# Six row-maximum tasks of attention A, one to a group instead of two in the third group

## The chip, the cores and the metric

The kernel runs on one core of a Trainium2 chip. The metric is the device time of one execution in microseconds (us). The kernel before was timed three times; the figure to beat or to miss is the median of those runs. Two runs of this kernel can be told apart when they differ by about 0.2%, or 3.9 us.

## The reference

Two attentions over the same input x (2048 tokens, 512 channels, 32 heads of 16) are mixed by a gate per token:

```python
q, k, v = heads(x @ wq), heads(x @ wk), heads(x @ wv)        # A, in 4 segments of 512 tokens
for s in range(4):
    logits = qs @ ks.T * scale + mask                        # causal inside the segment
    o = g * (phi(qs) @ M) / (phi(qs) @ z) + (1 - g) * softmax(logits) @ vs
    M, z = M + phi(ks).T @ vs, z + phi(ks).sum()             # memory of the segments before
a = concat(o) @ wo
b = softmax(q @ k.T * scale) @ v @ wob                       # B, its own weights, all 2048 keys
out = gate * a + (1 - gate) * b
```

The change touches only the two softmaxes, and in them only the row maxima that are taken off the logits before the exponential.

## The kernel before

**Units and slots.** After a stage of projections, the attention runs as 32 slots, k = 0 to 31. A slot holds one unit of B (number 32+k: four heads, 512 queries, all 2048 keys) and one unit of A (number k: four heads, one segment of 512 by 512, causal). It is written as 37 groups. Groups 0 to 31 are B's, groups 32 to 36 are A's five.

**What a group does.** `t_group` (L516) multiplies keys by queries into two PSUM banks (`tb`, `mb`; three banks in turn), and ScalarE takes the exponential of each into `raw` (L537); for A, GpSimd then clears the part above the diagonal (L540). A head pair takes rows 0 to 63 or rows 64 to 127 of TensorE's array, so two such matmuls in different halves run side by side. `pvs` (L856) then issues the multiplication of older exponentials by V into the bank `pvb` (`pv`, L543). `pvb` is shared: when a unit is finished its sums are copied out (`fin_copy`, L556) before the next unit's first `pv` may write there. B's sums are copied by ScalarE in group 33 (L562), A's by VectorE in group 0 of the slot after (L560).

**The maxima.** They must be known before a unit's exponentials, so they are found one slot ahead by multiplying queries by keys a second time and letting VectorE reduce the product. B's unit has 32 tasks `s_b` (L467), one between the two matmuls of each of 32 consecutive groups, from group 20 of one slot to group 19 of the next. Each makes two matmuls into one score tile and one reduction over 1024 values (L476). A's unit has six tasks `s_a` (L442), in the order of `ST_A`, with 512, 512, 384, 384, 256 and 128 keys; the last two take both head pairs at once. Each adds the causal mask by small matmuls (L456) and ends in one reduction (L460, or L462 for the last two). The task with 512 values in its reduction is called (0, None), the one before it (1, None).

**The two score tiles.** All tasks, `s_b` and `s_a`, take the two score tiles `sbk` in strict turn (`rot("s", SBK)`). So a task's matmuls have to wait until the reduction of the task two before it is done.

**Order.** Every engine runs its instructions in the order in which they are written. The table `plan` says which tasks a group gets; in the main loop a B group hands its tasks to `t_group`, which runs them between its two matmuls, and an A group runs them after `t_group` and before `pvs`. In slots 9 to 31, group 1 also holds one output projection `out_mm` (L615, 12 matmuls, L619); it has no `pv`. Slot 30 gives the last tasks for A; slot 31 has none.

```python
ST_A = [(3, 0), (3, 1), (2, 0), (2, 1), (1, None), (0, None)]      # L665
b = rot("s", SBK)                                                   # L445 in s_a, L471 in s_b
plan.setdefault((k, 2 * NT + n - (n > 2)), []).append(todo(s_a, k + 1, *t))   # L933, NT = 16
```

Of the kernel before, what the change touches and what calls it, by code (L numbers as in the profile page):

```python
# [23 lines left out]
NT = SEQ // 128  # L24
# [10 lines left out]
def gated_mix_kernel(ctx, tc, xt, wq, wk, wv, wo, beta, wqkv, wob, gate_w, out):  # L35
# [370 lines left out]
    def load_q(u):  # L406
        kd, qd, c = UN[u]
        load_qk(q_of(u), kd, 0, qd, c)

    def load_ka(u):  # L410
        kd, qd, c = UN[u]
        load_qk(KA[u % 2], kd, 1, qd, c)

    def load_kb(k, c=None):
        dst = KB[k % 3] if c is None else KB[k % 3][:, :, c * C:(c + 1) * C]
        load_qk(dst, "B", 1, k % 8, c)
# [6 lines left out]
    def load_vb(g):  # L423
        v_src(VB[g % 2], "B", g % 4, None)
# [55 lines left out]
    def m_chain(k):  # L480
        mx = pair_max(k)
        if k == 1:
            nc.vector.memset(mx[:, 0], 0.0)
        if k < 32:
            nc.vector.tensor_reduce(mx[:, 1], MXB.pop(32 + k).rearrange("q j p i c -> q (j p) i c"), axis=AX.X,
                                    op=OP.max)
        else:
            nc.vector.memset(mx[:, 1], 0.0)
        del MX[k]
        mx = mx.rearrange("q u h i -> q (u h i)")  # L490
        m8 = M8[k] = W.tile([128, 2, 32], FT, name="m8")
        hi = W.tile([128, 32], FR, name="mhi")
        nc.vector.tensor_scalar(hi, mx, -1.0, None, op0=OP.mult)
        nc.vector.tensor_copy(m8[:, 0], hi)
        nc.vector.scalar_tensor_tensor(m8[:, 1], mx, -1.0, hi, op0=OP.mult, op1=OP.subtract)
# [20 lines left out]
    def t_group(u, n, banks, between=()):  # L516


        kd, qd, c = UN[u]
        bs = [bank(banks) for _ in range(2)]  # L520
        c0 = 0
        for it, hs in (((n // 2, (n % 2 * 2, n % 2 * 2 + 1)),) if kd == "B" else GA[n]):
            q0 = 128 * it if kd == "A" else 0
            w = C - q0
            pn = it if kd == "B" else it % 2
            for j, h in enumerate(hs):
                if j:
                    for f in between:
                        f()
                r = slice(64 * j, 64 * j + 64)  # L530
                nc.tensor.matmul(bs[j][:, c0:c0 + w], k_of(u, h // 2)[r, 128 * it:128 * it + 128],  # L531
                                 q_of(u)[r, h // 2, q0:], start=True, stop=True)
                PT[u, it, h] = PTILE[pn % 2][:, 2 + j if (kd, it) == ("A", 2) else h][:, c0:c0 + w]
            c0 += w
        for j in range(2):
            pt = PTILE[pn % 2][:, 2 + j if (kd, n) == ("A", 4) else hs[j]]
            nc.scalar.activation(pt, bs[j], AF.Exp, scale=SCALE)  # L537
            if kd == "A":
                m = pt[:, :128] if n < 2 else pt.rearrange("p (a t) -> p a t", a=4)[:, ::3 if n < 4 else 2]
                nc.gpsimd.affine_select(out=m, in_=m, pattern=[[1, 128]] if n < 2 else [[0, 2], [1, 128]],  # L540
                                        compare_op=OP.is_ge, fill=0.0, base=0, channel_multiplier=-1)
# [119 lines left out]
    def todo(fn, *a):  # L661
        return lambda: fn(*a)
# [90 lines left out]
    for blk in range(16):  # L753
# [9 lines left out]
        n = blk + 1 + (c == 2)  # L763
# [74 lines left out]
    def late():  # L838
        proj.close()
        L = AT["L"] = ctx.enter_context(tc.tile_pool(name="late", bufs=1))  # L840
        VB[1] = L.tile([128, NT, 8, E + 1], FT, name="vb1")
        AT["o"] = [L.tile([128, 4, 2, C], FT, name=f"o{n}") for n in range(2)]
        AT["wh"] = L.tile([128, 4, 2, DM], FR, name="wh")
        AT["wl"] = L.tile([128, 4, 2, DM], FR, name="wl")
        AT["d"] = [L.tile([128, C], FT, name=f"d{n}") for n in range(2)]
        AT["oh"] = L.tile([128, 4, 2, 128], FR, name="oh")
        AT["ol"] = L.tile([128, 4, 2, 128], FR, name="ol")
        for p in range(2):
            set_aux(KB[2][:, p], 0)
# [4 lines left out]
    NG = 2 * NT + 5  # L854

    def pvs(k, n):  # L856

        ua, ub = k, 32 + k
        if n == 0:
            if k:  # L860
                pv(ua - 1, 2)
                fin_copy(ua - 1)
        elif k == 31 and n < 2 * NT:
            if n % 2 and n > 1:
                pv(ub, n // 2 - 1)
        elif 2 <= n < 2 * NT + 2:
            pv(ub, n // 2 - 1, n % 2 * 256, n % 2 * 256 + 256)
            if n == 2 * NT + 1:
                fin_copy(ub)
        elif n > 2 * NT + 1:  # L870
            m = n - 2 * NT - 2
            if m < 2:
                pv(ua, 0, 256 * m, 256 * m + 256)
            else:
                pv(ua, 1)
                pv(ua, 3)
# [13 lines left out]
    def beside(k, it):  # L890

        for f, it0, u in ((fin_load, NT + 1, 32 + k), (fin_rec, 5, 31 + k), (fin_bc, 6, 31 + k),
                          (fin_load, 1, k - 1), (fin_rec, 6, k - 1), (fin_bc, S_LAST + 2, k - 1)):
            if it == it0 and (k or it0 > NT):
                f(u)
        c, j = divmod(k - 1, 8)
        if k and j % 2:
            for kd, it0 in (("B", 9), ("A", 13)):
                if it == it0:
                    fin_norm(kd, j // 2, c)  # L900
        if k >= 8 and k % 2 == 0 and it == NT + 2:
            out_split(k // 8 - 1, k // 2 % 4)
        if (k, it) == (31, 4):
            grest = AT["grest"] = AT["o"][0][64:, 0, 0]
            nc.sync.dma_start(grest, GD[3 * C:].rearrange("(o t) -> o t", o=1).to_broadcast([64, C]))
        if (k, it) == (31, 9):
            grest = AT["grest"]
            nc.vector.tensor_scalar(grest, grest, nh[64:, 3:4], None, op0=OP.mult)
        if (k, it) == (31, NT + 2):
            fin_rec(63)  # L910
        if k == 31 and it == 13:
            o = AT["o"][1][:64, 3, 0]
            nc.gpsimd.tensor_tensor(o, o, AT["d"][0][:64], op=OP.mult)
        if k == 31 and it < 8 and it % 2 == 0:
            for a in range(2):
                tail_split(it // 2, slice(0, 3), a)
# [3 lines left out]
    plan = {}  # L920

    def spread(tasks, gs):
        for n, p in enumerate(gs):
            plan.setdefault(p, []).extend(tasks[len(tasks) * n // len(gs):len(tasks) * (n + 1) // len(gs)])

    for k in range(31):
        if k:
            spread([todo(s_b, 33 + k, *t) for t in (sorted(ST_B, key=lambda t: t[2]) if k == 1 else ST_B)],
                   [(k - 1, n) for n in range(2 * S_FIRST, 2 * NT)] + [(k, n) for n in range(2 * S_LAST)])
        else:  # L930
            spread(st33[EARLY:], sorted([(0, n) for n in range(2 * S_LAST)] + [(0, 2 * n) for n in range(4)]))
        for n, t in enumerate(ST_A):
            plan.setdefault((k, 2 * NT + n - (n > 2)), []).append(todo(s_a, k + 1, *t))  # L933

    for k in range(32):
        ua, ub = k, 32 + k
        banks = T3 + [b[:, 0] for b in SBK] * (k == 31)
        for n in range(NG):
            it = n // 2 if n < NG - 1 else NT + 2
            mid = plan.pop((k, n)) if n < 2 * NT and (k, n) in plan else []  # L940
            t_group(*(ub, n) if n < 2 * NT else (ua, n - 2 * NT), banks, mid)
            for f in plan.get((k, n), []) + ex[k][0].get(n, []):
                f()
            pvs(k, n)
            for f in ex[k][1].get(n, []):
                f()
            if n % 2 == 0 and n < NG - 1:
                continue
            beside(k, it)
            if it == S_LAST:  # L950
                m_chain(k + 1)
            if it == 4 and not k:
                late()
            if it == 4 and not k:
                load_q(ub + 2)
                for c in range(NC4):
                    load_kb(2, c)
            if it == NT and k < 29:
                load_q(ub + 3)
                load_kb(k + 3)  # L960
            if it == 6 and k < 31:
                load_q(ua + 1)
                load_ka(ua + 1)
                if (ua + 1) % 2 == 0:
                    load_va(ua + 1)
            if it == 9:
                if k % 2 == 0 and k < 30:
                    load_vb(k // 2 + 1)
                if 1 <= k <= 4:
                    load_wo(k - 1)  # L970
# [55 lines left out]
```

## Time and profile before

| | us |
|---|---|
| median of three runs | 1951.39 (1950.05 to 1952.76) |
| the profiled execution | 1949.85 |
| its span, first to last instruction | 1948.1 |
| TensorE busy | 1926.0 (99%) |
| VectorE busy | 1628.4 (84%) |
| ScalarE busy | 1436.2 (74%) |
| GpSimd busy | 277.0 (14%) |
| granted TensorE clock, mean | 0.997 |

Slots 1 to 8 last about 47.5 us each, slots 9 to 30 about 49.7 us. Matmuls are pipelined and their ends are modelled, so a busy TensorE may hide short waits; those are read from the start times of the instructions, and from the idle time of the weight loads (PEld), which the profile lists with the engine that ended it.

### The profile page before, as it was taken

The page shows a single profiled execution, that of the slowest core. Times are in us where ns is not written, and L with a number is a line of the kernel's source. Part 1 is how long each engine was busy: PE and PEld are TensorE (multiplying, and loading weights), DVE is VectorE, ACT ScalarE, POOL GpSimd, SP SyncE. Part 2 cuts the span into 40 slices and gives each one's busy share as a digit, 9 for nine tenths or more (in the row PEclk, how much of TensorE's full clock was granted, in tenths as well). Part 3 has the DMA queues.
Part 4 walks back from the last instruction along what each step waited for, and adds up shares of the span by engine and source line. Part 5 has one row for each costly group of instructions (what it writes and reads, how often), then busy time and mean ns, then how long its engine had stood idle before and what let it go on. Part 6 is the DMA issues. An engine that isn't in the chain of part 4 may idle for free.

```text
span 1948.1 us, 43539 instructions
## 1 busy us (share of the span) xinstructions
PE 1926.0 (99%) x17485; PEld 931.7 (48%) x17485; DVE 1628.4 (84%) x1798; ACT 1436.2 (74%) x2699; POOL 277.0 (14%) x497
## 2 busy tenths in 40 slices
PE   7999999999999999999999999999999999999999
PEld 5887777434444444444444444444444444444445
DVE  6135765899999999999999999999999999999942
ACT  4233333688888888888888888888888888888884
POOL 5200000011120101111111111111111111101022
PEclk9999999999999999999999999999999999999999
DMA  7666656744443445454544354534444444434111
GB/s 217 163 208 185 189 194 179 174 95 117 99 115 87 104 87 105 87 115 87 115 88 115 85 115 87 115 87 115 87 112 91 98 97 96 103 88 110 47 50 58
DMA packets 163790, 222.49 MB, mean 114 GB/s; under 512 B 39916, under 2 KB 90556, under 8 KB 157828
## 3 DMA queue, kind: packets, MB, share of 16 engines
q1 hardware_dynamic: 159284, 211.41, 44.0%
q0 software_dynamic: 3248, 8.03, 2.2%
q8 instruction: 138, 2.26, 0.5%
q14 instruction: 64, 0.52, 0.1%
q10 hardware_dynamic: 1056, 0.26, 0.1%
HBM read 147.95 MB, written 68.16 MB: 111 GB/s over the span
## 4 chain that ended last, share of the span: by engine, by line
PE 95%; DVE 2%; DMA 2%; SPq 0%; ACT 0%; issue 0%; DVEq 0%; ACTq 0%
PE pvb L553 33%; PE tb L531 17%; PE sbk L474 12%; PE mb L531 9%; PE tb L304 5%; PE sbk L452 3%; PE tb L619 2%; PE mb L304 2%; PE sbk L287 1%; PE tb L287 1%; PE pvb L304 1%; PE mb L619 1%; DMA pd<-pvs 1%; PE sbk L456 1%; PE mb L287 1%; PE pvb L287 1%
## 5 line engine op out<-in xcount | busy, mean ns | idle before, releaser
L476 DVE TENSOR_REDUCE mxb<-sbk 128x2 f32<-128x1024 f32 x1024 | 1222.0, 1222 | 57.7 <-PE sbk L474 25.4
L537 ACT ACTIVATE raw<-tb 128x512 f32<-128x512 f32 x1555 | 887.7, 598 | 147.3 <-PE tb L531 103.6
L553 PE MATMUL pvb<-raw,vb 128*17 128x256 f32 (+1 forms) x8072 | 639.9, 388 | 0.0
L537 ACT ACTIVATE raw<-mb 128x512 f32<-128x512 f32 x782 | 467.6, 598 | 73.0 <-PE mb L531 47.3
L474 PE MATMUL sbk<-xh,qb 64*128 64x512 f32 x1344 | 475.2, 445 | 2.9 <-DMA xh<-dB 2.0
L531 PE MATMUL tb<-qb,xh 64*128 64x512 f32 x872 | 353.2, 443 | 0.0
L553 PEld LDWEIGHTS pvb<-raw,vb 128*17 128x17 f32 x8072 | 134.9, 95 | 344.0 <-issue 338.7
L474 PE MATMUL sbk<-kb,qb 64*128 64x512 f32 x704 | 239.4, 444 | 0.2 <-DVE mxb L476 0.2
L531 PEld LDWEIGHTS tb<-qb,xh 64*128 64x128 f32 x872 | 146.4, 185 | 176.6 <-issue 89.7
L540 POOL TENSOR_SCALAR_AFFINE_SELECT raw<-raw 128x256 f32<-128x256 f32 (+1 forms) x320 | 116.1, 363 | 694.8 <-ACT raw L537 687.0
L531 PE MATMUL mb<-qb,xh 64*128 64x512 f32 x445 | 198.8, 447 | 0.0
L474 PEld LDWEIGHTS sbk<-xh,qb 64*128 64x128 f32 x1344 | 189.1, 185 | 8.0 <-DVE mxb L476 4.3
L531 PE MATMUL tb<-qb,kb 64*128 64x512 f32 x470 | 191.9, 446 | 0.8 <-DVE st L314 0.8
L460 DVE TENSOR_REDUCE mx<-sbk 128x2 f32<-128x768 f32 (+1 forms) x128 | 136.7, 1090 | 22.9 <-PE sbk L456 18.5
L531 PEld LDWEIGHTS mb<-qb,xh 64*128 64x128 f32 x445 | 82.1, 184 | 94.9 <-issue 50.8
L531 PEld LDWEIGHTS tb<-qb,kb 64*128 64x128 f32 x470 | 79.2, 184 | 98.9 <-issue 53.1
L593 POOL TENSOR_TENSOR o<-o,d 128x512 f32<-128x512 f32 x31 | 39.8, 1284 | 549.1 <-DMA d<-rd 505.0
L531 PE MATMUL mb<-qb,kb 64*128 64x512 f32 x234 | 104.0, 445 | 0.0
L474 PEld LDWEIGHTS sbk<-kb,qb 64*128 64x128 f32 x704 | 95.2, 184 | 5.7 <-issue 3.2
L553 PE MATMUL pvb<-raw,va 128*17 128x256 f32 (+2 forms) x1280 | 94.7, 384 | 0.8 <-ACT pvs L562 0.8
L452 PE MATMUL sbk<-ka,qa 64*128 64x256 f32 (+3 forms) x512 | 87.9, 358 | 1.1
L311 ACT ACTIVATE st<-tb 128x512 fp32r<-128x512 f32 x33 | 19.8, 599 | 82.5 <-DVE phi L310 45.5
(284 smaller groups left out, 1851.5 us busy)
## 6 DMA issues: line engine op xcount, KB each, us to landing
xh<-dB SPq DMA_DIRECT2D x38, 512.0 KB
vb<-vdB SPq DMA_DIRECT2D x16, 1088.0 KB
dB<-st SPq DMA_DIRECT2D x64, 256.0 KB
dA<-st SPq DMA_DIRECT2D x64, 256.0 KB
pd<-pvs SPq DMA_DIRECT2D x64, 256.0 KB
kb<-dB SPq DMA_DIRECT2D x22, 512.0 KB
xh<-dB SPq DMA_DIRECT2D x38, 256.0 KB
qb<-dB SPq DMA_DIRECT2D x64, 128.0 KB
```

Source lines behind the costliest of these rows:

```text
L287: nc.tensor.matmul(b, lhs, WV[wi][:, k, :], start=n == 0, stop=n == 11)
L304: nc.tensor.matmul(b, WS[ws][w][wi][:, k, :], (XH, XL)[xi][c][:, k, :], start=n == 0, stop=n == 11)
L452: nc.tensor.matmul(b[:, j, c0:c0 + n], q_of(u)[r, p, i * 128:(i + 1) * 128], k_of(u, p)[r, :n], start=True, stop=False)
L460: nc.vector.tensor_reduce(m[:, :, p, i], b[:, :, :n], axis=AX.X, op=OP.max)
L474: nc.tensor.matmul(b[:, j], q_of(u)[r, p, i * 128:(i + 1) * 128], k_of(u, p)[r, kc * C:(kc + 1) * C], start=True, stop=True)
L476: nc.vector.tensor_reduce(MXB[u][:, :, p, i, kc], b, axis=AX.X, op=OP.max)
L531: nc.tensor.matmul(bs[j][:, c0:c0 + w], k_of(u, h // 2)[r, 128 * it:128 * it + 128], q_of(u)[r, h // 2, q0:], start=True, stop=True)
L537: nc.scalar.activation(pt, bs[j], AF.Exp, scale=SCALE)
L540: nc.gpsimd.affine_select(out=m, in_=m, pattern=[[1, 128]] if n < 2 else [[0, 2], [1, 128]], compare_op=OP.is_ge, fill=0.0, base=0, channe ...
L553: nc.tensor.matmul(PVB[32 * h:32 * h + E + 1, q0 + lo:q0 + hi], vt[:, it, 4 * q + h, :], pt[:, lo:hi], start=it == 0 and lo == 0, stop=it ...
L593: nc.gpsimd.tensor_tensor(o, o, d, op=OP.mult)
L619: nc.tensor.matmul(b, (AT["oh"], AT["ol"])[oi][:, g, a], (AT["wh"], AT["wl"])[wi][:, g, a], start=n == 0, stop=n == 11)
```

## The change

A's six tasks of a slot were put into groups 32, 33, 34, 34, 35, 36. Now they go into 32, 33, 34, 35, 36 and group 0 of the next slot, for the slots 0 to 29; slot 30 keeps the old places. A B group may thus hold two tasks. It hands only the last one of its list to `t_group`; the rest run after `t_group`. In group 0 the last of the list is the `s_b` task, so `s_a`'s (0, None) follows it. Where a group of slot 0 holds two `s_b` tasks (groups 0, 2, 4, 6, 7 and 19), they now run in the other order, one between the two matmuls and one behind them.

```diff
         for n, t in enumerate(ST_A):
-            plan.setdefault((k, 2 * NT + n - (n > 2)), []).append(todo(s_a, k + 1, *t))
+            at = (k, 2 * NT + n - (n > 2)) if k == 30 else divmod(k * NG + 2 * NT + n, NG)
+            plan.setdefault(at, []).append(todo(s_a, k + 1, *t))
...
-            mid = plan.pop((k, n)) if n < 2 * NT and (k, n) in plan else []
+            mid = [plan[k, n].pop()] if n < 2 * NT and (k, n) in plan else []
```

On TensorE in group 34 of slot 13, before, from the last matmul of `t_group` to the start of group 35 (`sbk_114` and `sbk_115` are the two score tiles, `va` is V of A; the mask's matmuls are left out):

```order
L531 MATMUL mb<-qa_74,ka_72 128x128
L452 MATMUL sbk_114<-ka_71,qa_73 128x384 x2
...
L452 MATMUL sbk_115<-ka_71,qa_73 128x384 x2
...
L553 MATMUL pvb<-raw_86,va_76 17x256 x4
L531 MATMUL tb_111<-qa_74,ka_72 128x384
```

The same place in the changed kernel, on to the first matmuls of group 35's task:

```order
L531 MATMUL mb<-qa_74,ka_72 128x128
L452 MATMUL sbk_114<-ka_71,qa_73 128x384 x2
...
L553 MATMUL pvb<-raw_86,va_76 17x256 x4
L531 MATMUL tb_111<-qa_74,ka_72 128x384
...
L452 MATMUL sbk_115<-ka_71,qa_73 128x384 x2
```

The second task has moved behind the first `pv` of A and behind group 35's score matmuls; the two after it move on by one group each.

On TensorE at the start of slot 14, before, from the end of group 36 to the output projection in group 1:

```order
L553 MATMUL pvb<-raw_86,va_76 17x128 x4
L531 MATMUL tb_110<-qb_69,xh_88 128x512
L474 MATMUL sbk_114<-kb_89,qb_70 128x512 x2
L531 MATMUL mb<-qb_69,xh_88 128x512
L553 MATMUL pvb<-raw_86,va_76 17x256 x4
L531 MATMUL tb_111<-qb_69,xh_88 128x512
L474 MATMUL sbk_115<-kb_89,qb_70 128x512 x2
L531 MATMUL tb_110<-qb_69,xh_88 128x512
L619 MATMUL mb<-wh,oh 128x512 x4
```

And in the changed kernel, where L452 on `ka_71` is the task (0, None) that came over:

```order
L553 MATMUL pvb<-raw_86,va_76 17x128 x4
L531 MATMUL tb_110<-qb_69,xh_88 128x512
L474 MATMUL sbk_115<-kb_89,qb_70 128x512 x2
L531 MATMUL mb<-qb_69,xh_88 128x512
L452 MATMUL sbk_114<-ka_71,qa_73 128x128 x2
...
L553 MATMUL pvb<-raw_86,va_76 17x256 x4
L531 MATMUL tb_111<-qb_69,xh_88 128x512
L474 MATMUL sbk_115<-kb_89,qb_70 128x512 x2
L531 MATMUL tb_110<-qb_69,xh_88 128x512
L619 MATMUL mb<-wh,oh 128x512 x4
```

Group 0 has two tasks, and the `s_b` tasks of groups 0 and 1 now take the same score tile (`sbk_115`), with only (0, None) between them; before, they took different ones.

On VectorE at the start of a slot, as the difference (L462 into `mx` is A's reduction, L476 into `mxb` is B's, L560 copies A's finished sums out of `pvb`):

```order
 L462 TENSOR_REDUCE mx<-sbk_114 128x4
-L462 TENSOR_REDUCE mx<-sbk_115 128x4
-L476 TENSOR_REDUCE mxb<-sbk_114 128x2
+L476 TENSOR_REDUCE mxb<-sbk_115 128x2
+L462 TENSOR_REDUCE mx<-sbk_114 128x4
 L560 COPY pvs<-pvb 128x512
 L476 TENSOR_REDUCE mxb<-sbk_115 128x2
```

The last reduction of A's tasks has moved behind the first of B's in the next slot and stands directly ahead of the copy. The orders of ScalarE, GpSimd and the DMA queues are the same in both kernels.

## The prediction

> **What bounds the kernel now.** I read the page first, then the groups of instructions, then two whole slots as windows, and last the timelines of single engines around one slot boundary. The page:
>
> ```profile
> PE 1926.0 (99%) x17485; PEld 931.7 (48%) x17485; DVE 1628.4 (84%) x1798; ACT 1436.2 (74%) x2699; POOL 277.0 (14%) x497
> PE 95%; DVE 2%; DMA 2%; SPq 0%; ACT 0%; issue 0%; DVEq 0%; ACTq 0%
> ```
>
> TensorE (PE) is busy throughout and carries 95% of the chain that ended last. Two slots as windows (columns: length, then busy time of PE, PEld, VectorE, ScalarE, GpSimd), slot 13 first, then slot 3:
>
> ```profile
> 982.98:1032.71 49.73, 49.70 (x508) 20.90 (x505) 46.10 (x47) 42.05 (x78) 6.02 (x12) 1.00 0.38 84
> 498.33:545.79 47.46, 47.42 (x497) 19.15 (x494) 45.73 (x47) 40.76 (x76) 7.35 (x15) 1.00 0.48 99
> ```
>
> VectorE (DVE) works 46.10 of 49.73 us in slot 13, but 45.73 of 47.46 in slot 3, which has no output projection: there the two engines are almost level. So the question is only where TensorE waits for VectorE. The groups of weight loads tell how much of that there is:
>
> ```profile
> L452 PEld LDWEIGHTS sbk<-ka,qa 64*128 64x128 f32 x512 | 52.1, 185 | 5.9 <-DVE mx L460 4.2 <-issue 0.9
> L474 PEld LDWEIGHTS sbk<-xh,qb 64*128 64x128 f32 x1344 | 189.1, 185 | 8.0 <-DVE mxb L476 4.3 <-DMA xh<-dB 2.3 <-issue 0.6
> ```
>
> A's tasks wait 4.2 us in all for a reduction of A (L460), about 0.14 in each of the 31 slots that hold tasks; that is what the change can take away. B's tasks (L474) wait 4.3 us for one of B in this group.
>
> **The boundary of slots 13 and 14.** The rows of TensorE that begin a step (start, length, instruction), groups 34, 35, 36 of slot 13 and 0, 1 of slot 14, which start at 1027.58, 1029.43, 1030.94, 1032.71 and 1033.93:
>
> ```profile
> 1027.58 0.44 PE L531 MATMUL tb<-qa,ka 64*128 64x384 f32 x1
> ...
> 1028.15 0.23 PE L456 MATMUL sbk<-cmask,crows 64*128 64x64 bf16 x4
> 1028.42 0.45 PE L452 MATMUL sbk<-ka,qa 64*128 64x384 f32 x2
> 1028.71 0.23 PE L456 MATMUL sbk<-cmask,crows 64*128 64x64 bf16 x4
> 1028.87 0.63 PE L553 MATMUL pvb<-raw,va 128*17 128x256 f32 x8
> 1029.43 0.50 PE L531 MATMUL tb<-qa,ka 64*128 64x384 f32 x4
> ...
> 1030.38 0.63 PE L553 MATMUL pvb<-raw,va 128*17 128x256 f32 x8
> 1030.94 0.38 PE L531 MATMUL mb<-qa,ka 64*128 64x256 f32 x1
> ...
> 1031.28 0.22 PE L452 MATMUL sbk<-ka,qa 64*128 64x128 f32 x2
> ...
> 1031.72 1.06 PE L553 MATMUL pvb<-raw,va 128*17 128x384 f32 x16
> 1032.71 0.49 PE L531 MATMUL tb<-qb,xh 64*128 64x512 f32 x1
> ...
> 1033.37 0.63 PE L553 MATMUL pvb<-raw,va 128*17 128x256 f32 x8
> 1033.93 0.50 PE L531 MATMUL tb<-qb,xh 64*128 64x512 f32 x1
> ...
> 1034.59 0.50 PE L619 MATMUL mb<-wh,oh 128*128 128x512 f32 x1
> ```
>
> What VectorE, ScalarE and GpSimd do there:
>
> ```profile
> 1033.47 1.23 DVE L476 TENSOR_REDUCE mxb<-sbk 128x2 f32<-128x1024 f32 x1 [0.94 <-PE mb L531]
> 1027.85 0.60 ACT L562 ACTIVATE pvs<-pvb 128x512 f32<-128x512 f32 x1
> 1030.69 0.90 POOL L540 TENSOR_SCALAR_AFFINE_SELECT raw<-raw 128x256 f32<-128x256 f32 x2 [0.78 <-ACT raw L537]
> ```
>
> **Groups 34 to 36 get shorter by 0.42 us.** From the mask's matmuls to `pv` it is 0.16 (1028.71 to 1028.87). Without its second task group 34 could therefore start `pv` at 1028.15 + 0.16 = 1028.31 rather than 1028.87. But this `pv` is A's first write to `pvb`, and ScalarE copies B's sums out until 1027.85 + 0.60 = 1028.45. With 0.05 for the hand-over (below) it starts at 1028.50: 0.37 gained, and 0.19 of what the task and its wait cost is not. The copy hangs on exponentials of group 33, which the change does not move, so I take 1028.50; 1028.31 is the other end. Group 35 lasts 1.51 now; with the (2, 1) task it is as group 34 with one task and no wait, 0.73 to `pv` (1027.58 to 1028.31) and 0.56 for it (1028.87 to 1029.43): 1.29, a gain of 0.22. Group 36 gets (1, None): 0.95 to `pv`, as now in group 35 (1029.43 to 1030.38), and 0.99 for it (1031.72 to 1032.71): 1.94 instead of 1.77, a loss of 0.17. Together -0.37 - 0.22 + 0.17 = -0.42. A possible new wait: `pv` of group 36 needs GpSimd's work on group 35, which ends at 1030.69 + 0.90 = 1031.59, 2.16 after that group's start; `pv` comes 1.29 + 0.95 = 2.24 after it. It holds by 0.08, now by 0.13, so I count nothing, and 0.15 as the upper end.
>
> **Group 0 gets longer by 0.44.** (0, None) costs 0.44 in group 36 now, from its first matmul to `pv` (1031.28 to 1031.72), with its tile free; its tile is free in group 0 too, since (1, None) will have been reduced long before. Group 0 goes from 1.22 to 1.66.
>
> **Group 1 gets a new wait.** Its `s_b` task now takes the tile of group 0's `s_b`. That reduction runs from 0.76 after the slot's start (1033.47 - 1032.71) to 0.76 + 1.23 = 1.99, and nothing can start it sooner: it follows its own matmuls. Group 1 starts at 1.66. Before, this task had the other tile, free already. What such a wait costs can be seen in slot 3, which starts at 498.33 and has no projection in group 1, so that TensorE runs into VectorE in groups 2 and 3:
>
> ```profile
> 500.38 0.51 PE L474 MATMUL sbk<-xh,qb 64*128 64x512 f32 x2
> 500.79 0.49 PE L531 MATMUL tb<-qb,kb 64*128 64x512 f32 x1
> ...
> 501.82 0.50 PE L531 MATMUL mb<-qb,kb 64*128 64x512 f32 x1
> 502.11 0.50 PE L474 MATMUL sbk<-xh,qb 64*128 64x512 f32 x2
> 502.44 0.39 PE L531 MATMUL tb<-qb,kb 64*128 64x512 f32 x1
> 502.77 0.63 PE L553 MATMUL pvb<-raw,vb 128*17 128x256 f32 x8
> ```
> ```profile
> 499.10 1.23 DVE L476 TENSOR_REDUCE mxb<-sbk 128x2 f32<-128x1024 f32 x1 [0.94 <-PE tb L531]
> 500.24 0.68 DVE L560 COPY pvs<-pvb 128x512 f32<-128x512 f32 x1
> 500.83 3.48 DVE L476 TENSOR_REDUCE mxb<-sbk 128x2 f32<-128x1024 f32 x3
> ```
>
> The first reduction ends at 500.33, the waiting task starts at 500.38: a hand-over of 0.05. In the next group the task starts at 502.11, the group's second score matmul 0.33 later and what follows another 0.33 later: queued behind the wait are the second score matmul and all that comes after. So in group 1 the task starts at 1.99 + 0.05 = 2.04 and the group ends at 2.70. Without a wait it would last 0.66 as now (1033.93 to 1034.59) and end at 2.32. The new wait costs 0.38, and nothing covers it, since what stands behind it, the projection, is TensorE's own work.
>
> **Slots 9 to 30 (22 of them):** -0.42 + 0.44 + 0.38 = +0.40 each, 8.8 us.
>
> **Slots 1 to 8.** They have no projection, and from group 2 on VectorE sets the pace. Three of its reductions that follow each other take 3.48, so (3.48 - 1.23) / 2 = 1.13 from start to start; each begins about 0.09 before the one ahead of it is over. A reduction of 512 values:
>
> ```profile
> L462 DVE TENSOR_REDUCE mx<-sbk x2: 693/960/1226, 1030.5 to 1031.8; 128x4 f32<-128x1024 f32 x1, 128x4 f32<-128x512 f32 x1
> ```
>
> 0.69, less the overlap of 0.09, puts 0.60 into VectorE's queue ahead of the copy. The reduction of group 1's task starts 0.60 later after the slot's start, and group 3's task, which waits for it (502.11, the reduction begun at 500.83 being over), does too; from there the slot goes on as before. TensorE's own waits in groups 1 and 2 lie inside these 0.60. Net 0.60 - 0.42 = +0.18 each, 1.4 us for eight. The ends are 0 (if `pv` of group 34 starts at 1028.31) and 0.33 (with a wait of 0.15 in group 36).
> [...]
>
> **Slot 0** only has six pairs of tasks in another order; the matmuls and reductions are the same and the projections of V between them leave VectorE time. Zero, give or take 0.5. Slot 31 and the tail are untouched.
>
> **The sum:** 8.8 + 1.4 = +10.2 us: 1960.1 on the profiled execution's 1949.85, which lies 1.5 below the median; on the median, 1951.4 + 10.2 = 1961.6.
>
> **The rivals.**
> *The wait is filled.* If TensorE took the second score matmul while group 1's task waits, that would run at 1.66 + 0.33 = 1.99, the task from 2.04 to 2.37, and the wait would cost 0.05. Slots 9 to 30 would lose 0.07 each, 1.5 us, and with 1.4 from slots 1 to 8 the time would be 1954.3, no change by the bound of 0.2% (3.9 us) that a measurement can tell here. Against it: in slot 3 the second matmul (500.79, 502.44) comes after the task that waited. 7%.
> [...]
>
> *Faster.* The wait in group 34 goes and none comes: 0.14 in 30 slots, -4.2 us, 1947.2. For that group 0's reduction must be over when group 1 starts, by 1.66 after the slot's start rather than 1.99, and `pv` of group 34 must not wait for the copy. For it: the idle time before L452, which is real. Against it: the order of the tiles, and 0.76 + 1.23. 5%.
>
> *More waits.* ScalarE and GpSimd, pressed closer in groups 34 to 36, hold `pv` or the score banks by 0.15 or more in every slot: 30 x 0.15 = 4.5 more, 1966.1. For it: only 0.08 of slack. Against it: GpSimd's row above begins after 0.78 of idling, so it is not behind. 8%.
>
> **How the numbers follow.** My forecast has 80%. Its low end is `pv` of group 34 without the copy's hold: 8.8 - 22 x 0.19 = 4.6 and nothing from slots 1 to 8, 1956.0. Its high end is 10.2 + 4.5, 1966.1. That range leaves out the two first rivals and half of the third. Faster 5%, the same 7%, slower 88%.
>
> **What would show it.** Right: in the changed kernel's timeline group 1's L474 starts about 2.04 after the slot, L619 at 2.70; `pv` of group 34 starts just after L562; slots 9 to 30 last about 50.13 instead of 49.73 us, slots 1 to 8 about 47.64; the idle time before L452 (4.2 us) is nearly gone and that before L474 put down to L476 has grown by some 8 us. Wrong: if group 1's L474 starts at once, or L531 comes ahead of it, or if slots 9 to 30 keep their length.

## The result, and the profile after

The changed kernel takes 1959.34 us, the median of six runs (1957.45 to 1962.84); six runs of the kernel before give 1949.82 (1946.91 to 1952.76). The ratio is 1.0053, with an interval from 1.0041 to 1.0065: about 10.3 us slower by the ratio, 9.5 by the two medians, where 10.2 were forecast. The profiled execution took 1958.30 us, with a span of 1956.6.

The page, the lines that answer to those shown of before:

```profile
PE 1928.7 (99%) x17485; PEld 934.4 (48%) x17485; DVE 1629.0 (83%) x1798; ACT 1439.2 (74%) x2699; POOL 275.2 (14%) x497
PE 94%; ACT 2%; DVE 2%; issue 1%; DMA 0%; SPq 0%; ACTq 0%; DVEq 0%
```

These lines hardly tell the two kernels apart: there are as many instructions, and TensorE is as busy. Its busy time grew by 2.7 us, and the span by 8.5. The slots as windows, slot 13 and slot 3:

```profile
982.95:1033.10 50.15, 49.93 (x510) 21.01 (x506) 46.09 (x48) 42.07 (x78) 5.97 (x12) 1.00 0.40 83
495.78:543.72 47.94, 47.73 (x498) 19.24 (x494) 45.99 (x48) 40.99 (x76) 7.35 (x15) 1.00 0.43 100
```

Slot 13 went from 49.73 to 50.15. From the start of slot 9 to that of slot 31 the trace shows 1092.99 us before and 1103.24 after: the whole loss of 10.2 us lies there. Slots 1 to 8 lose 1.1 in all and slot 0 gains 1.1; the remaining difference between the two spans, 1.8 less after, lies ahead of slot 0, in work that the change does not touch.

The groups of weight loads: first L474 on `kb` before, then three groups after; last the idle time before L474 from the waits of the window 782.24 to 1885.48, which is slots 9 to 30 (us, times):

```profile
L474 PEld LDWEIGHTS sbk<-kb,qb 64*128 64x128 f32 x704 | 95.2, 184 | 5.7 <-issue 3.2 <-DVE mxb L476 1.2 <-DVE recm L342 0.4
```
```profile
L452 PEld LDWEIGHTS sbk<-ka,qa 64*128 64x128 f32 x512 | 52.2, 185 | 4.5 <-issue 0.9 <-DVE mx L460 0.2
L474 PEld LDWEIGHTS sbk<-xh,qb 64*128 64x128 f32 x1344 | 187.1, 185 | 14.5 <-DVE mxb L476 9.1 <-DMA xh<-dB 2.3 <-DVE mx L462 1.5
L474 PEld LDWEIGHTS sbk<-kb,qb 64*128 64x128 f32 x704 | 94.2, 184 | 8.6 <-issue 3.4 <-DVE mxb L476 3.1 <-DVE mx L462 0.9
```
```profile
  DVE mxb L476: 6.5, 22
```

The wait of A's tasks, 4.2 us before, is down to 0.2. In its place stand 22 waits of 0.3 us for a reduction of B, one in each of the 22 slots with a projection; the same view of before lists not one there. In slots 1 to 8 there are eight new waits for L462, the reduction of (0, None), 1.5 + 0.9 = 2.4 us.

The timeline of TensorE at the boundary of slots 13 and 14. Groups 34, 35 and 36 start at 1028.34, 1029.92 and 1031.21, the new slot at 1033.10, its group 1 at 1034.66:

```profile
1028.34 0.44 PE L531 MATMUL tb<-qa,ka 64*128 64x384 f32 x1
1028.92 0.23 PE L456 MATMUL sbk<-cmask,crows 64*128 64x64 bf16 x4
1029.37 0.63 PE L553 MATMUL pvb<-raw,va 128*17 128x256 f32 x8 [0.22 <-ACT pvs L562]
1029.92 0.50 PE L531 MATMUL tb<-qa,ka 64*128 64x384 f32 x4
1031.21 0.38 PE L531 MATMUL mb<-qa,ka 64*128 64x256 f32 x1
1032.11 1.06 PE L553 MATMUL pvb<-raw,va 128*17 128x384 f32 x16
1033.10 0.49 PE L531 MATMUL tb<-qb,xh 64*128 64x512 f32 x1
1033.43 0.39 PE L531 MATMUL mb<-qb,xh 64*128 64x512 f32 x1
1033.66 0.22 PE L452 MATMUL sbk<-ka,qa 64*128 64x128 f32 x2
1034.10 0.63 PE L553 MATMUL pvb<-raw,va 128*17 128x256 f32 x8
1034.66 0.50 PE L531 MATMUL tb<-qb,xh 64*128 64x512 f32 x1
1035.14 0.50 PE L474 MATMUL sbk<-kb,qb 64*128 64x512 f32 x2
1035.80 0.50 PE L619 MATMUL mb<-wh,oh 128*128 128x512 f32 x1
```

ScalarE's copy in group 34, and VectorE at the start of slot 14:

```profile
1028.62 0.60 ACT L562 ACTIVATE pvs<-pvb 128x512 f32<-128x512 f32 x1
1033.86 1.23 DVE L476 TENSOR_REDUCE mxb<-sbk 128x2 f32<-128x1024 f32 x1 [0.41 <-PE sbk L474]
1035.00 0.68 DVE L462 TENSOR_REDUCE mx<-sbk 128x4 f32<-128x512 f32 x1
```

Two things are to be seen. In group 34 `pv` now waits for ScalarE, 0.22 us of idling before it: the wait for VectorE has gone and the copy behind it shows. In group 1 the task starts at 1035.14, 2.04 after the slot, when the reduction that began at 1033.86 is over at 1035.09; the projection follows at 2.70.

In numbers, the change in the mean length of each group, in slots 9 to 29: group 0 +0.35, group 1 +0.46, group 34 -0.26, group 35 -0.22, group 36 +0.12, all others within 0.01. Together this is +0.45 a slot. Slot 30 keeps A's old places and gains nothing there: its groups 0 and 1 get longer by 0.34 and 0.44, and no other group changes.

### The profile page after: what moved, and what is told of

Read it like the earlier page. It is cut to its first block, busy times and chain, and to the rows that moved or that the text cites. A ratio compares the mean times of both kernels' runs of the same rounds, so it can differ in the third digit from the quotient of the medians.

```text
span 1956.6 us, 43539 instructions
## 1 busy us (share of the span) xinstructions
PE 1928.7 (99%) x17485; PEld 934.4 (48%) x17485; DVE 1629.0 (83%) x1798; ACT 1439.2 (74%) x2699; POOL 275.2 (14%) x497
## 4 chain that ended last, share of the span: by engine, by line
PE 94%; ACT 2%; DVE 2%; issue 1%; DMA 0%; SPq 0%; ACTq 0%; DVEq 0%
PE pvb L553 33%; PE tb L531 18%; PE sbk L474 12%; PE mb L531 9%; PE tb L304 4%; PE tb L619 2%; PE mb L304 2%; PE sbk L452 2%; PE sbk L287 1%; PE tb L287 1%; PE pvb L304 1%; PE mb L619 1%; ACT raw L537 1%; PE mb L287 1%; PE pvb L287 1%
## 5 line engine op out<-in xcount | busy, mean ns | idle before, releaser
L476 DVE TENSOR_REDUCE mxb<-sbk 128x2 f32<-128x1024 f32 x1024 | 1222.2, 1222 | 44.1 <-PE sbk L474 32.3
L474 PE MATMUL sbk<-xh,qb 64*128 64x512 f32 x1344 | 470.6, 447 | 2.8 <-DMA xh<-dB 2.0
L531 PE MATMUL tb<-qb,xh 64*128 64x512 f32 x872 | 353.8, 443 | 0.0
L474 PE MATMUL sbk<-kb,qb 64*128 64x512 f32 x704 | 237.2, 446 | 0.0
L531 PEld LDWEIGHTS tb<-qb,xh 64*128 64x128 f32 x872 | 146.7, 185 | 174.3 <-issue 90.5
L531 PE MATMUL mb<-qb,xh 64*128 64x512 f32 x445 | 198.9, 447 | 0.0
L474 PEld LDWEIGHTS sbk<-xh,qb 64*128 64x128 f32 x1344 | 187.1, 185 | 14.5 <-DVE mxb L476 9.1
L531 PE MATMUL tb<-qb,kb 64*128 64x512 f32 x470 | 191.8, 446 | 0.8 <-DVE st L314 0.8
L531 PEld LDWEIGHTS mb<-qb,xh 64*128 64x128 f32 x445 | 82.1, 184 | 94.9 <-issue 50.8
L531 PEld LDWEIGHTS tb<-qb,kb 64*128 64x128 f32 x470 | 79.2, 184 | 98.1 <-issue 52.6
L531 PE MATMUL mb<-qb,kb 64*128 64x512 f32 x234 | 104.0, 445 | 0.0
L474 PEld LDWEIGHTS sbk<-kb,qb 64*128 64x128 f32 x704 | 94.2, 184 | 8.6 <-issue 3.4
L452 PE MATMUL sbk<-ka,qa 64*128 64x256 f32 (+3 forms) x512 | 84.7, 346 | 0.0
```

Source lines behind the costliest of these rows:

```text
L452: nc.tensor.matmul(b[:, j, c0:c0 + n], q_of(u)[r, p, i * 128:(i + 1) * 128], k_of(u, p)[r, :n], start=True, stop=False)
L474: nc.tensor.matmul(b[:, j], q_of(u)[r, p, i * 128:(i + 1) * 128], k_of(u, p)[r, kc * C:(kc + 1) * C], start=True, stop=True)
L476: nc.vector.tensor_reduce(MXB[u][:, :, p, i, kc], b, axis=AX.X, op=OP.max)
```

## The experiments

Each ratio is to runs of the kernel before that were timed with the experiment: a median of 1949.48 us for the first four, of 1950.01 for the others.

**The new wait alone: (0, None) in the middle of group 0, `s_b` behind it.** Then group 1's task takes the tile of (0, None) instead of that of `s_b`; all else is as in the changed kernel.

```diff
-            mid = [plan[k, n].pop()] if n < 2 * NT and (k, n) in plan else []
+            mid = [plan[k, n].pop(0 if k else -1)] if n < 2 * NT and (k, n) in plan else []
```

> The changed kernel, but in group 0 of slots 1 to 30 the task (0, None) runs between the two score matmuls and B's task behind them. Group 0 does the same work, group 1's task of B again gets the tile of (0, None), whose reduction is short and early. Theory (turn of the tiles): no wait in group 1, L619 at 1.57 + 0.66 = 2.23 after the slot's start instead of 2.70, so slots 9 to 30 stand within 0.1 us of the kernel before; slots 1 to 8 stay about 0.2 longer, since VectorE's queue is as long. In all about +1 us against the kernel before, ratio 1.0005. Rival (the added task in group 0 itself, by delaying A's last pv and VectorE's copy L560): the loss stays, ratio 1.005.

Measured: 1953.54 us, ratio 1.0022 (1.0013 to 1.0032). Slot 14 starts at 1036.92 in this kernel:

```profile
1036.92 0.50 PE L531 MATMUL tb<-qb,xh 64*128 64x512 f32 x1
1037.38 0.48 PE L531 MATMUL mb<-qb,xh 64*128 64x512 f32 x1
1038.58 0.49 PE L531 MATMUL tb<-qb,xh 64*128 64x512 f32 x1
1038.58 0.73 PE L474 MATMUL sbk<-kb,qb 64*128 64x512 f32 x2
1039.24 0.50 PE L619 MATMUL mb<-wh,oh 128*128 128x512 f32 x1
```

Group 1's task starts with the group, and the projection 0.66 after that: the wait is gone from all of slots 9 to 30, and with it more than half of the loss. So the turn of the two tiles made it, and the rival that priced this kernel at 1.005 falls. The size is a miss all the same: about +1 us was expected and +4.1 measured. Group 0 lasts 1.66, 0.44 more than before, against 0.35 in the changed kernel, and A's three groups give back only 0.35; what is left is +0.10 in each of slots 9 to 29, where the theory had nothing. Slots 1 to 8 lose 0.36 each (the median) instead of 0.2: their groups 0 to 3 get 0.71 longer together, against 0.60 in the changed kernel, and where the 0.11 comes from stays open.

**A's side alone: the sixth task stays in group 36.** On the kernel before:

```diff
-            plan.setdefault((k, 2 * NT + n - (n > 2)), []).append(todo(s_a, k + 1, *t))
+            plan.setdefault((k, 2 * NT + min(n, 4)), []).append(todo(s_a, k + 1, *t))
```

> The kernel before, but the six tasks go to groups 32, 33, 34, 35, 36, 36: only A's side of the change, nothing at the slot's start. Theory: group 34 loses its wait (0.14) but its pv now waits for ScalarE's copy of pvb, so A's groups gain nothing: -0.02 to +0.07 us a slot, -0.6 to +2.2 us in all, ratio 0.9997 to 1.0011. Rival (the wait in group 34 was a real loss): -0.14 in 31 slots, -4.3 us, ratio 0.998.

Measured: 1953.02 us, ratio 1.0014 (1.0006 to 1.0023). Groups 34 and 35 get shorter by 0.26 and 0.22, group 36 gets longer by 0.55. Idle time before L452, and group 34:

```profile
L452 PEld LDWEIGHTS sbk<-ka,qa 64*128 64x128 f32 x512 | 52.2, 186 | 1.0 <-issue 0.9
```
```profile
1028.65 0.44 PE L531 MATMUL tb<-qa,ka 64*128 64x384 f32 x1
1029.67 0.63 PE L553 MATMUL pvb<-raw,va 128*17 128x256 f32 x8 [0.22 <-ACT pvs L562]
1028.92 0.60 ACT L562 ACTIVATE pvs<-pvb 128x512 f32<-128x512 f32 x1
```

The 4.2 us of waiting are gone and the kernel is no faster: the price of the task moved two groups on, and `pv` waits for the copy instead. The time came out just above the range expected (1.0011), group 34 having gained 0.11 a slot less than expected; the rival that had this kernel faster (0.998) falls.

**The wait at group 1's end.** On the changed kernel, group 1's task goes behind both score matmuls instead of between them:

```diff
-            mid = [plan[k, n].pop()] if n < 2 * NT and (k, n) in plan else []
+            mid = [plan[k, n].pop()] if n < 2 * NT and (k, n) in plan and not (k and n == 1) else []
```

> The changed kernel, but group 1 of slots 1 to 30 runs its task of B behind its two score matmuls instead of between them. The task still waits for the reduction of group 0's task, to 2.04 after the slot's start. Theory (a wait in the middle also holds back the second score matmul, which then runs alone): L619 at 2.38 instead of 2.70 in slots 9 to 30, so 22 x 0.32 = 7.0 us less than the changed kernel, nothing in slots 1 to 8: ratio 1.0015 against the kernel before. Rival (only the wait counts): no gain, ratio 1.005.

Measured: 1955.43 us, ratio 1.0024 (1.0014 to 1.0035). Group 1 of slot 14, a slot that starts at 1034.54:

```profile
1036.10 0.50 PE L531 MATMUL tb<-qb,xh 64*128 64x512 f32 x2
1036.59 0.51 PE L474 MATMUL sbk<-kb,qb 64*128 64x512 f32 x2
1037.02 0.50 PE L619 MATMUL mb<-wh,oh 128*128 128x512 f32 x1
```

The task still starts 2.05 after the slot, held by the same reduction, but now with one matmul less queued behind it: the projection starts at 2.48 instead of 2.70. That is 0.22 a slot, not the 0.32 expected. The second score matmul now runs beside the first (two of L531 at 1036.10, both in 0.50) and no longer by itself behind the task, which saves its 0.33 (1035.47 to 1035.80 in the changed kernel); but the projection, which takes all 128 rows, comes 0.43 after the task's two matmuls (1036.59 to 1037.02), where a score matmul came 0.33 after them (1035.14 to 1035.47). What stands behind a wait is thus a part of its price, here about half: group 1 is 0.24 longer than in the kernel before, instead of 0.46. The rival, by which only the wait counts (1.005), falls.

**Which task waits in group 34: the two orders of `ST_A`.** Both on the kernel before, with its places. First the short tasks ahead:

```diff
-    ST_A = [(3, 0), (3, 1), (2, 0), (2, 1), (1, None), (0, None)]
+    ST_A = [(2, 0), (2, 1), (3, 0), (3, 1), (1, None), (0, None)]
```

> The kernel before, but with A's tasks in the order (2, 0), (2, 1), (3, 0), (3, 1), (1, None), (0, None), still two in group 34. The task of group 33 then has a reduction of 0.96 us instead of 1.23, so the tile is free when the second task of group 34 comes; and with two tasks pv comes later than the copy of pvb. Theory: the wait of 0.14 us goes and no other takes its place: -4.3 us, ratio 0.998. Rival (pv of group 34 is held by the copy, or by GpSimd, in any case): same time, ratio 1.000.

Measured: 1947.68 us, ratio 0.9991 (0.9982 to 1.0000), a miss: the wait did not go but moved. The idle time before L452, and where it now lies (group 35 starts at 1026.99):

```profile
L452 PEld LDWEIGHTS sbk<-ka,qa 64*128 64x128 f32 x512 | 52.4, 186 | 5.7 <-DVE mx L460 4.6 <-issue 0.9
```
```profile
1026.99 0.50 PE L531 MATMUL tb<-qa,ka 64*128 64x384 f32 x4
1027.44 0.18 PEld L452 LDWEIGHTS sbk<-ka,qa 64*128 64x128 f32 x2 [0.15 <-DVE mx L460]
1026.16 2.36 DVE L460 TENSOR_REDUCE mx<-sbk 128x2 f32<-128x1024 f32 x2 [0.39 <-PE sbk L456]
```

Group 34 gains 0.10 and group 35 loses 0.16: the two long reductions, 2.36 for both, now stand in group 34, and the task of group 35 waits for the first of them, which is over at about 1026.16 + 1.23 = 1027.39, 0.05 before the task starts. So a long reduction must not be the last but one ahead of a task that follows soon. This gives the next order: a short task ahead of the pair, and a short one as its first.

```diff
-    ST_A = [(3, 0), (3, 1), (2, 0), (2, 1), (1, None), (0, None)]
+    ST_A = [(3, 0), (2, 0), (2, 1), (3, 1), (1, None), (0, None)]
```

> The kernel before, but with A's tasks in the order (3, 0), (2, 0), (2, 1), (3, 1), (1, None), (0, None), two in group 34 as before. With the short tasks first the wait of group 34 only moved to group 35, behind the 1.23 us reduction of (3, 0). Now the tasks on which groups 34 and 35 wait, the second and the third, both have reductions of 0.96. Theory (turn of the tiles): no wait in 34 nor in 35; group 33 0.06 shorter, group 34 0.06 longer for the longer task and 0.22 shorter for the wait, group 35 as before: -0.2 us a slot, -6.8 us in all, ratio 0.9965. Rival (pv of group 34 is held by ScalarE's copy or GpSimd's select at about the old time): group 34 stays at 1.75 or more, -2 us or less, ratio 0.999.

Measured: 1941.72 us, ratio 0.9958 (0.9945 to 0.9972), faster than both kernels.

```profile
L452 PEld LDWEIGHTS sbk<-ka,qa 64*128 64x128 f32 x512 | 52.5, 186 | 1.0 <-issue 0.9
```
```profile
1028.93 0.44 PE L531 MATMUL tb<-qa,ka 64*128 64x384 f32 x1
1029.27 0.40 PE L452 MATMUL sbk<-ka,qa 64*128 64x384 f32 x2
1029.58 0.48 PE L452 MATMUL sbk<-ka,qa 64*128 64x512 f32 x2
1030.06 0.63 PE L553 MATMUL pvb<-raw,va 128*17 128x256 f32 x8
1030.62 0.50 PE L531 MATMUL tb<-qa,ka 64*128 64x384 f32 x4
```

In group 34 the second task follows the first by 0.31 and nothing waits. The group lasts 1.69, 0.16 less than before; group 33 lasts 0.06 less, having a task with 384 keys in place of 512, and no other group changes. 31 x 0.22 = 6.8 us, as expected and inside the interval (5.5 to 10.7). A task with 512 keys costs 0.06 more than one with 384, as group 33 shows, so the wait itself was worth 0.22, more than the 0.14 of idle time that the weight loads show. The kernel with the short tasks first says the same of its group 34: two longer tasks and no wait, 0.12 - 0.22 = -0.10. This order takes the wait away without moving a task to another group, and so without changing the turn of the tiles at the next slot's start.

**The same order with the changed kernel's task rule,** which alone acts in slot 0 here:

```diff
-    ST_A = [(3, 0), (3, 1), (2, 0), (2, 1), (1, None), (0, None)]
+    ST_A = [(3, 0), (2, 0), (2, 1), (3, 1), (1, None), (0, None)]
...
-            mid = plan.pop((k, n)) if n < 2 * NT and (k, n) in plan else []
+            mid = [plan[k, n].pop()] if n < 2 * NT and (k, n) in plan else []
```

> The order (3, 0), (2, 0), (2, 1), (3, 1), (1, None), (0, None), and besides the changed kernel's rule for slot 0 alone: of two tasks in a B group one runs between the score matmuls, the other behind them. If the gain of 0.24 us in each of groups 2, 4 and 6 of slot 0 comes from that rule, it is there again: 0.7 us less than with the order alone, ratio 0.996. Rival (those groups gained from something else in the changed kernel): as with the order alone.

Measured: 1942.62 us, ratio 0.9961 (0.9949 to 0.9974), not to be told from the kernel without the rule, so the times cannot decide. The trace does: groups 2, 4 and 6 of slot 0 are shorter by 0.25, 0.23 and 0.25, as in the changed kernel (group 19 is 0.24 shorter and group 20 as much longer in both). Group 6, in the kernel before and then in the changed one; L304 is the projection behind the tasks:

```profile
357.64 1.41 PE L474 MATMUL sbk<-xh,qb 64*128 64x512 f32 x4
358.82 0.39 PE L531 MATMUL mb<-qb,kb 64*128 64x512 f32 x1
359.14 2.12 PE L304 MATMUL tb<-xh,wv 128*128 128x512 f32 x8
```
```profile
355.34 0.50 PE L531 MATMUL tb<-qb,kb 64*128 64x512 f32 x1
355.68 0.38 PE L531 MATMUL mb<-qb,kb 64*128 64x512 f32 x1
356.18 0.50 PE L474 MATMUL sbk<-xh,qb 64*128 64x512 f32 x2
356.60 2.12 PE L304 MATMUL tb<-xh,wv 128*128 128x512 f32 x8
```

The task that waits starts 0.84 after the group in both (356.18 now). The second score matmul stands ahead of it now, 0.34 after the group's start instead of 1.18, beside the first task's second matmul. So the projection follows the waiting task by 0.42 and starts at 1.26 instead of 1.50: the step of the third experiment again, with the same size.

**Short tasks first, one to a group:** does the copy hold `pv` of group 34 also with another order?

> The kernel before with the tasks (2, 0), (2, 1), (3, 0), (3, 1), (1, None), (0, None) in groups 32, 33, 34, 35, 36, 36. Group 34 then has one task of 512 keys instead of 384. Theory (its pv is held by ScalarE's copy): group 34 lasts 1.57 us as in the changed kernel, whatever its task; groups 32 and 33 0.06 shorter, 35 about 0.06 longer. Rival (something in the task holds it): group 34 gets 0.06 longer, 1.63.

Timed once, 1955.21 us, so only its trace is read. Group 34 here (it starts at 1029.59 and the next at 1031.22):

```profile
1029.59 0.44 PE L531 MATMUL tb<-qa,ka 64*128 64x384 f32 x1
1030.67 0.63 PE L553 MATMUL pvb<-raw,va 128*17 128x256 f32 x8 [0.21 <-ACT pvs L562]
1029.92 0.60 ACT L562 ACTIVATE pvs<-pvb 128x512 f32<-128x512 f32 x1
```

The group lasts 1.63, the rival's number, but not for the rival's reason: group 33 lasts 0.05 less (1.24 against 1.29 with the sixth task in group 36), and the two together 2.87 in both kernels. `pv` starts 0.15 after the copy's end (1030.52) here and there (1029.52, then 1029.67). The copy holds it, and the copy is tied to group 33, not 34. My expectation took the length of group 34 by itself and could not have told the two apart.

## Why the prediction was right

**Group 34: too much.** Forecast -0.37, measured -0.26. The step that failed is the hand-over: I took 0.05, the time from VectorE's reduction to a task of L474 (500.33 to 500.38 in the kernel before), for the one from ScalarE's copy to `pv`. In the changed kernel the copy ends at 1028.62 + 0.60 = 1029.22 and `pv` starts at 1029.37, 0.15 later, and so in two more kernels. That the copy takes over as the holder was right: GpSimd's last work on the exponentials of group 33, which `pv` needs too, is over earlier, at 1028.86 + 0.29 = 1029.15.

```profile
1028.86 0.29 POOL L540 TENSOR_SCALAR_AFFINE_SELECT raw<-raw 128x128 f32<-128x128 f32 x1 [0.20 <-ACT raw L537]
L553 PEldq EVENT_SEMAPHORE  x1: 51/51/51, 1029.3 to 1029.3; - x1
```

The second line shows what the 0.15 is made of. `pv` waits for ScalarE in an instruction of its own on TensorE, which starts at 1029.26, 0.04 after the copy, and takes 51 ns; then come `pv`'s weight load at 1029.34 and its matmul at 1029.37. In group 1 the weight load of L474 waits for VectorE itself, and it starts at 1035.14, 0.05 after the reduction (1035.09). In the kernel before the instruction of `pv` ran at 1028.49, again 0.04 after the copy (1028.45), while the second task still stood ahead of `pv`, and cost nothing.

**Groups 35 and 36: right.** -0.22 as forecast, and +0.12 for +0.17. Group 36 was shorter because its task took 0.90 to `pv` (1031.21 to 1032.11) instead of 0.95. GpSimd did not hold `pv` there, but it came closer than I had worked out: its row on group 35 ended at 1031.18 + 0.90 = 1032.08, 0.03 before `pv` and not 0.08.

**Group 0: too much.** +0.35 for +0.44. I had taken the time from the task's first matmul to `pv` in group 36 for its price, as if `pv` could otherwise start where the task does. That time is 0.44 here too (1033.66 to 1034.10). But the task's first matmul comes 0.23 after the second score matmul (1033.43), where `pv` came 0.32 after it in the kernel before (1033.05 to 1033.37): 0.23 + 0.44 - 0.32 = 0.35.

```profile
1033.05 0.39 PE L531 MATMUL mb<-qb,xh 64*128 64x512 f32 x1
```

The first weight load of L452 here, at 1033.50, lies inside the row of the score matmul (1033.43 to 1033.82, its end modelled), and so does its first matmul, at 1033.66. Where the same task stands between the two score matmuls, as in the first experiment, it costs the full 0.44.

**Group 1: right in place, and its error undid the one above.** The task started at 2.04 and the projection at 2.70, both as forecast. The wait ends at a time that the slot's first reduction sets, so what group 0 did not cost was waited for in group 1: +0.46 for +0.38. Groups 0 and 1 together: +0.81 for +0.82.

**The sum of slots 9 to 30: right, with a slip in it.** Slots 9 to 29 lost +0.45 each for +0.40. Slot 30 keeps A's old places, so nothing is gained there and it lost 0.79; I had counted it like the others. Together 21 x 0.45 + 0.79 = 10.2 us for 8.8. Of the 1.4 between them, the hand-over makes 21 x 0.11 = 2.3 and slot 30 0.4; the cheaper group 36 takes back 1.1 and groups 0 and 1 0.2.

**Slots 1 to 8: right.** The typical slot lost 0.22 (0.18 forecast). Groups 0 to 3 together got longer by 0.60, the time that (0, None)'s reduction was to put into VectorE's queue, and A's groups gave back 0.36 instead of 0.42. The eight together lost only 1.1, because group 16 was 0.15 to 0.51 longer than usual in slots 1, 6 and 8 of the profiled execution of before; why there is not known.

**Slot 0: missed.** Zero was forecast; groups 2, 4 and 6 gain 0.24 each, 0.72 in all. I counted matmuls and reductions, which are the same, and not what stands behind a task that waits. I had used that very step for group 1. With A's own gain at the end of slot 0, 0.35, which my sum left out, it comes to 1.1.

**The total: partly luck.** Against the forecast, slots 9 to 30 were 1.4 worse, slots 1 to 8 0.3 and slot 0 1.1 better, so the misses cancelled. Two of them are slips of about 0.4 with opposite signs: A's gain was counted in slot 30, which has none, and not in slot 0, which has it. The sign and the larger terms do not hang on this; that the total came out within 0.1 us does.

**The rivals.** "The wait is filled" fell: the second score matmul follows the task that waits (1035.47 after 1035.14). "Faster" fell on both of its conditions, the turn of the tiles and the copy. "More waits" was half there, the copy's hold being longer by 0.1, but not at 0.15 in every slot and not through GpSimd. The idle time before L474 put down to L476 was to grow by some 8 us; it grew by 12.2 - 5.5 = 6.7 (9.1 + 3.1 after, 4.3 + 1.2 before), and 2.4 more are put down to L462.

## What to carry to other kernels

Where tasks take two buffers in turn, one task more at a place changes the partner of every task behind it: before moving one, write down for the next two or three which reduction each has to wait for, when that ends, and what is queued behind the wait. A wait that goes shows the next holder at the same place (here a copy), so price that one too before counting the gain. The order of the tasks was the better lever: with a short reduction where the next user of the tile comes soon, the wait went and nothing came in its place.

## What the runs showed of the hardware

- From the end of ScalarE's copy to the first matmul into the buffer that it read: 0.15 us in three kernels (1029.22 to 1029.37, 1029.52 to 1029.67, 1030.52 to 1030.67). In the changed kernel the wait there is an instruction of its own on TensorE (at 1029.26, 51 ns), with the weight load behind it (1029.34). From VectorE's reduction to a task of L474, whose weight load waits by itself: 0.05 (1035.09 to 1035.14 in the changed kernel, 500.33 to 500.38 in the one before).
- The same small task cost 0.35 us behind a pair of score matmuls (group 0 of the changed kernel) and 0.44 between them (group 0 of the first experiment).
- Idle time of the weight loads understated a wait: the 0.14 before L452 in group 34 was worth 0.22 of the group's length, by the order (3, 0), (2, 0), (2, 1), (3, 1).
- Two matmuls with 64 rows each, for the two heads of a pair, started together: both of L531 at 1028.65, with 0.44 us each (group 34, sixth task in group 36).
- In slot 14 of the changed kernel the profile shows matmuls with 64 rows with 0.50 us behind `pv`, which takes all rows (1034.66), with 0.50 behind a wait (1035.14), and with 0.39 behind others of 64 rows (1033.43). These ends are modelled, the starts are not: a score matmul came 0.33 after a pair that waited (1035.14 to 1035.47), and the projection again 0.33 behind it (1035.80). With all 128 rows and directly behind such a pair, a projection came 0.43 or 0.42 later (1036.59 to 1037.02 in the third experiment, 356.18 to 356.60 in slot 0 of the changed kernel).
